# The dummy matmuls that wake TensorE's clock read a preamble constant instead of a zero tile, and are one more

## Chip, cores and metric

One core of a Trainium2 chip. The metric is the device time of one execution in microseconds (us). Every execution also has a span, from the first to the last instruction of the program; it is about 1.8 us shorter than the time.

## The reference, cut

```python
def _A_ref(x, k_cache, v_cache, wq, wo):     # x (1,2048,640); 32 heads of 192; window W = 512
    q = (x @ wq).reshape(B, Sq, Hq, Dh).transpose(0, 2, 1, 3)
    k, v = k_cache[:, :, Sk-W:, :], v_cache[:, :, Sk-W:, :]
    p = softmax(einsum("bhqd,bhkd->bhqk", q, k) * Dh**-0.5)
    return einsum("bhqk,bhkd->bhqd", p, v)...reshape(B, Sq, Hq*Dh) @ wo

def _B_ref(x, w_gate, w_up, w_down):         # 640 -> 1536 -> 640
    return (silu(x @ w_gate) * (x @ w_up)) @ w_down

xn = layernorm(A_x)
return A_x + _A_ref(xn, ...) * silu(_B_ref(xn, ...))
```

## The kernel before

It runs the FFN first, then attention. The FFN's first 512 rows come in four row tiles of 128 (tile 0 to tile 3). A tile's way is: load x, mean and variance on VectorE (two `bn_stats` and a `bn_aggr`), square root on ScalarE, reciprocal and normalisation on VectorE, five transposes on PE, two copies out of PSUM on ScalarE, 30 matmuls of 128 columns. `keep_warm` keeps PE busy in front of that with matmuls whose result is overwritten.

```python
zero_t = ffw.tile([P, 512], bf, name="zero_t")
nc.vector.memset(zero_t[:], 0.0)
...
load_x(0, (nc.scalar, nc.sync))              # a half on each queue
load_x(1, (nc.scalar,))
load_first(slice(0, 2), (nc.sync, nc.scalar))   # gate and up weights, chunks 0-1 of 5
load_first(slice(2, NC))                        # chunks 2-4: "second gate/up weights"
load_x(2, (nc.scalar,))
...
def keep_warm(n, cols=512):
    for _ in range(n):
        nc.tensor.matmul(
            first[2][1][:, 0:cols], zero_t[:, 0:P], zero_t[:, 0:cols], start=True, stop=True
        )

keep_warm(9)
keep_warm(6, P)
...
ln_stats(0)
ln_sqrt(0)
ln_stats(1, lambda: ln_apply(0, (slice(0, 2 * P), slice(2 * P, D))))
ready(0)                                     # transposes and copies of tile 0
...
for t in range(4):
    ...                                      # 30 matmuls per tile; after the first 21 of them:
                    if t < 2:
                        ln_stats(t + 2, lambda: ln_apply(t + 1))
                    ...
                    ready(t + 1)             # transposes of the next tile
```

VectorE, ScalarE and PE each keep this order: the statistics of tile 2 begin before the normalisation of tile 1, and tile 1's transposes stand behind 21 of tile 0's matmuls.

The softmax here doesn't subtract the row's maximum and nothing guards it: scores larger than these inputs give would overflow.

## Time and profile before

| | before |
|---|---|
| median of the time, first 3 runs | 920.73 us (920.32 to 921.08) |
| span of the profiled run | 919.1 us |
| PE busy | 99% of the span |
| first dummy / first real matmul | 1.23 / 6.57 us |
| tile 1's transposes (start of the unbroken stretch) | 8.54 us |

A row of the timeline is start, duration, engine, line, operation, operands, count, and in brackets the idle time before it with what ended it. A row of the chain is start, duration, what. In these rows PE is TensorE, PEld its weight loads, DVE VectorE, ACT ScalarE, SP SyncE and POOL GpSimd; a q behind a name means its queue or sequencer. x_t is a tile of x, stats, mv and rstd are its statistics, xn the normalised tile, tp its transposes in PSUM, xnT the copy of them, wg_sb and wu_sb the gate and up weights, sc and gu their products. Cold and warm stand for TensorE's slow and fast clock, as told apart by how far matmuls start from each other. The prediction shows the lines of before.

### The profile page before, as it was taken

How to read it: one execution, taken by the hardware profiler on the slowest of the kernel's cores; microseconds unless marked ns; L12 is line 12 of the kernel's file. 1: busy time of each engine (PE TensorE's matmuls, PEld its weight loads, DVE VectorE, ACT ScalarE, POOL GpSimd, SP SyncE). 2: the span in 40 equal slices, each digit the busy share in tenths (PEclk: the TensorE clock that was granted, in tenths of full speed). 3: DMA queues.
4: the chain of work that ended last, by engine and by line, in shares of the span. 5: the costliest groups of instructions: out<-in, count | busy, mean ns of one | idle time of the engine just before them, and what ended most of it. 6: DMA issues, size and time to landing. Idle time of an engine off the chain costs nothing.

```text
span 919.1 us, 23152 instructions
## 1 busy us (share of the span) xinstructions
PE 912.6 (99%) x9898; PEld 548.9 (60%) x9920; DVE 601.7 (65%) x844; ACT 474.4 (52%) x840; POOL 85.3 (9%) x269
## 2 busy tenths in 40 slices
PE   9999999999999999999999999999999999999998
PEld 6444444465757575656565656666666666665665
DVE  6443321467777777777777777676867777777657
ACT  4222222556464656565656565655555555556471
POOL 0000000000000000000000000000000000001976
PEclk9999999999999999999999999999999999999999
DMA  9412430045352544263534343435243444343526
GB/s 302 76 34 65 90 84 1 1 75 113 54 113 49 112 51 107 54 109 54 109 58 109 57 109 52 109 54 107 56 85 76 88 79 78 87 71 102 118 61 166
DMA packets 248166, 77.53 MB, mean 84 GB/s; under 512 B 228992, under 2 KB 248064, under 8 KB 248064
## 3 DMA queue, kind: packets, MB, share of 16 engines
q1 hardware_dynamic: 245696, 73.39, 39.5%
q10 hardware_dynamic: 2368, 2.67, 0.9%
q8 instruction: 77, 1.26, 0.6%
q14 instruction: 25, 0.20, 0.1%
HBM read 38.93 MB, written 2.62 MB: 45 GB/s over the span
## 4 chain that ended last, share of the span: by engine, by line
PE 99%; DMA 1%; DVE 0%; ACTq 0%; issue 0%
PE mm L448 22%; PE sc L462 18%; PE mm L487 16%; PE sc L602 15%; PE sc L282 11%; PE mm L312 6%; PE sc L572 4%; PE sc L564 2%; PE mm L539 2%; PE mm L564 1%; DMA x_t<-in_A_x_dram 1%; PE gu L282 0%; PE mm L321 0%; PE sc L539 0%; PE sc L487 0%
## 5 line engine op out<-in xcount | busy, mean ns | idle before, releaser
L466 ACT ACTIVATE p_t<-sc 128x1024 bf16<-128x1024 f32 x254 | 253.0, 1023 | 120.3 <-PE sc L462 120.3
L453 DVE TENSOR_REDUCE qT<-mm 128x512 bf16<-128x1024 f32 x189 | 231.2, 1223 | 99.0 <-PE mm L448 96.5
L517 ACT ACTIVATE O_b<-mm,r 128x192 bf16<-128x192 f32 x486 | 165.0, 422 | 183.1 <-issue 136.6
L448 PE MATMUL mm<-xnT,wq_p 64*128 64x512 bf16 x1890 | 237.5, 376 | 0.0
L462 PE MATMUL sc<-qT,khat 64*128 64x512 bf16 x1524 | 198.0, 376 | 0.0
L487 PEld LDWEIGHTS <-p_t 64*128 64x128 bf16 x3584 | 159.0, 94 | 33.8
L487 PE MATMUL mm<-V_p,p_t 64*128 64x193 bf16 x3520 | 176.4, 243 | 0.0
L615 DVE TENSOR_TENSOR s_m<-s_m,sc 128x1024 f32<-128x1024 f32 x108 | 131.9, 1221 | 60.7 <-PE sc L602 52.3
L602 PE MATMUL sc<-wo_p,OT_b 64*128 64x512 bf16 x1296 | 168.9, 376 | 0.0
L448 PEld LDWEIGHTS <-wq_p 64*128 64x128 bf16 x1890 | 105.0, 94 | 98.9 <-issue 0.8
L462 PEld LDWEIGHTS <-khat 64*128 64x128 bf16 x1536 | 85.3, 94 | 80.4 <-DVE s_t L615 0.3
L602 PEld LDWEIGHTS <-OT_b 64*128 64x128 bf16 x1296 | 70.3, 94 | 44.1 <-issue 0.3
L615 DVE TENSOR_TENSOR s_t<-s_t,sc 128x512 f32<-128x512 f32 x108 | 74.2, 687 | 28.4 <-PE sc L572 26.6
L589 POOL MEMSET turn_t<- 128x1 f32 x220 | 21.6, 98 | 700.0 <-PE mm L487 506.0
L290 DVE TENSOR_TENSOR hT<-sc,sg 128x512 bf16<-128x512 f32 x46 | 31.7, 692 | 81.5 <-ACT sg L289 81.5
L289 ACT ACTIVATE sg<-sc 128x512 bf16<-128x512 f32 x46 | 27.3, 596 | 69.8 <-PE sc L282 66.7
L282 PE MATMUL sc<-xnT,wg_sb 128*128 128x512 bf16 (+1 forms) x255 | 60.1, 354 | 0.5
L282 PE MATMUL sc<-xnT,wu_sb 128*128 128x512 bf16 (+1 forms) x255 | 59.5, 355 | 0.2
L572 PE MATMUL sc<-OT_b,wo_p 64*128 64x512 bf16 (+1 forms) x345 | 50.3, 376 | 0.0
L312 PE MATMUL mm<-wd_sb,hT 128*128 128x512 bf16 x189 | 43.6, 379 | 0.2
L282 PEld LDWEIGHTS <-wu_sb 128*128 128x128 bf16 x285 | 27.1, 98 | 26.8 <-issue 0.3
L282 PEld LDWEIGHTS <-wg_sb 128*128 128x128 bf16 x285 | 27.2, 98 | 26.3
(83 smaller groups left out, 418.3 us busy)
## 6 DMA issues: line engine op xcount, KB each, us to landing
wo_p<-in_A_wo_dram SPq DMA_DIRECT2D x16, 480.0 KB, 4.7
K_p<-in_A_k_cache_dram SPq DMA_DIRECT2D x32, 192.0 KB, 4.4
V_p<-in_A_v_cache_dram SPq DMA_DIRECT2D x32, 192.0 KB, 3.3
wq_p<-in_A_wq_dram SPq DMA_DIRECT2D x64, 80.0 KB, 2.8
wq_p<-in_A_wq_dram SPq DMA_DIRECT2D x16, 160.0 KB, 3.0
x_t<-in_A_x_dram SPq DMA_DIRECT2D x13, 160.0 KB, 3.0
x_b<-in_A_x_dram SPq DMA_DIRECT2D x4, 512.0 KB, 6.1
OT_b<-O_b SPq DMA_TRANSPOSE x124, 2.8
```

Of the source, the lines that this page charges most:

```text
L282: nc.tensor.matmul(out, w_sb[:, c, f * P : (f + 1) * P], xnT[:, c, qc], start=(c == 0), stop=(c == NC - 1),)
L290: nc.vector.tensor_tensor(hTs[b][:, f, :], u, sg[:], ALU.mult)
L312: nc.tensor.matmul(dn, at, by, start=(f == 0), stop=(f == NF - 1))
L448: nc.tensor.matmul(q_ps[:, h, :], pairs[pr]["wq"][r, c, j * P : (j + 1) * P], xnT[r, c, b * 512 : (b + 1) * 512], start=(c == 0), stop=(c ...
L453: nc.vector.reduce_sum(qTs[i][:, j, :], q_ps[:, :, :].rearrange("p h n -> p n h"), axis=AX.X)
L462: nc.tensor.matmul(sc[:, h, :], khat[r, j, ks], qT[r, j, :], start=(j == 0), stop=(j == 2))
L466: nc.scalar.activation(p_t[:, :, :], sc[:, :, :], ACT.Exp, scale=scale)
L487: m = nc.tensor.matmul(acc[:, k, h * 256 : h * 256 + Dh + 1], Ps[i][kc][r, h, qt * P : (qt + 1) * P], V_p[r, kc, h, 0 : Dh + 1], start=(p ...
L517: nc.scalar.activation(O_b[:, qt, h, :], a_k[:, h, 0:Dh], ACT.Copy, scale=r[:, k, h, :])
L572: nc.tensor.matmul(ps.rearrange("p (t q) -> p t q", q=P), pairs[i // NB]["wo"][r, j, MC:D], OTs[i][:, :, :].rearrange("p (t j) q -> p j t ...
L602: m = nc.tensor.matmul(ps[:, k, :], OTs[i][r, 3 * (2 * half + k) + j, :], pairs[i // NB]["wo"][r, j, MAIN], start=(turn == 0 and j == 0), ...
L615: nc.vector.tensor_tensor(to, to, ps, ALU.add)
```

## The change

Its intent: PE need not wait for VectorE's fill, so it can begin to be busy some 0.4 us sooner and its clock is raised sooner; the tenth dummy fills the time won.

```diff
-        zero_t = ffw.tile([P, 512], bf, name="zero_t")
-        nc.vector.memset(zero_t[:], 0.0)
...
         def keep_warm(n, cols=512):
+            ones = [nc.const_aps.tensor(1.0, (P, k), bf) for k in (P, cols)]
             for _ in range(n):
-                nc.tensor.matmul(
-                    first[2][1][:, 0:cols], zero_t[:, 0:P], zero_t[:, 0:cols], start=True, stop=True
-                )
-
-        keep_warm(9)
+                nc.tensor.matmul(first[2][1][:, 0:cols], *ones, start=True, stop=True)
+
+        keep_warm(10)
         keep_warm(6, P)
```

The constant is one bf16 1.0 per partition; a matmul reads it with a step of 0 along its columns, as weights and as moving data.

## The prediction

> **What bounds the kernel now.** I read the page first (busy shares, slices, chain), then the chain over the first 40 us in order of time, then the timeline of the first 9 us, engine by engine, and last a table of two-microsecond windows. The page says that TensorE is the bound of the whole:
>
> ```profile
> PE 912.6 (99%) x9898; PEld 548.9 (60%) x9920; DVE 601.7 (65%) x844; ACT 474.4 (52%) x840; POOL 85.3 (9%) x269
> ...
> PE 99%; DMA 1%; DVE 0%; ACTq 0%; issue 0%
> ```
>
> 99% of the chain that ended last is PE and 1% (some 5 us) is a DMA. So two things can move the end: less matmul work in the body, which the change doesn't touch, or an earlier start of the unbroken stretch of matmuls. The change lies wholly in the first 6 us, so the question is what sets that start. The chain in order of time answers it:
>
> ```profile
> 0.72 0.56 ACTq L188
> ...
> 1.32 0.60 ACTq L188
> ...
> 1.94 0.45 ACTq L193
> ...
> 2.42 4.99 DMA x_t<-in_A_x_dram
> ...
> 7.44 0.49 DVE stats L243
> 7.94 0.07 DVE rstd L265
> ...
> 8.03 0.46 DVE xn L267
> ...
> 8.54 0.45 PE tp L335 x5
> ```
>
> Up to 8.54 us no matmul stands in this chain, neither the dummies nor the first row tile's real ones. It is ScalarE's queue issuing loads, the load of row tile 2 from 2.42 to 7.42 us, the statistics of that tile, and then, because VectorE takes them in this program order, the normalisation of tile 1, which the five transposes at 8.54 wait for. From there PE runs without a break that matters. The timeline of PE shows the slack in front of that point:
>
> ```profile
> 1.23 4.66 PE L230 MATMUL gu<-zero_t 128*128 128x512 bf16 x15 [1.23 <-DVE zero_t L176]
> 5.68 0.74 PE L335 MATMUL tp<-ident,xn 128*128 128x128 bf16 x5
> 6.57 0.27 PE L282 MATMUL sc<-xnT,wg_sb 128*128 128x128 bf16 x1
> ...
> 7.85 0.22 PE L282 MATMUL gu<-xnT,wg_sb 128*128 128x128 bf16 x1
> 8.54 0.45 PE L335 MATMUL tp<-ident,xn 128*128 128x128 bf16 x5 [0.46 <-DVE xn L267]
> ```
>
> The dummies end where tile 0's transposes begin (5.68); tile 0's first 21 matmuls run from 6.57 to 7.85 + 0.22 = 8.07; then PE idles 0.46 us. Anything that PE does sooner or later before 8.07 is first absorbed there.
>
> **What the Trainium skill says.** "TensorE: Matmul & The Clock Gate", Part 1: the array's clock is halved until a free-running window of about 3.4 us has seen it busy, and back-to-back matmuls then go from N/1.2 to N/2.4 + 2.5 ns (427 to 216 ns at 512 columns, 107 to 56 at 128). The trace agrees on the pitches: the dummies' weight loads start at 1.63, 2.06, 2.48 and so on to 5.04, eight steps of 0.426 us, and the first real matmuls start at 6.62, 6.73, 6.84 (0.11 apart), then from 7.02 on 7.07, 7.13, 7.18 (0.055 apart). So the clock was cold through all fifteen dummies and went up at about 6.9 us, some 5.7 us after the first. That is what the dummies are for. The granted clock that the windows print (1.00 throughout) doesn't show this gate; the pitch does. The same page, "Weight-path perf modes": fast weight load asks for 128 weights, an input that isn't FP32, and a column step between -1,023 and 1,024 elements. A broadcast constant has step 0 and stays inside this; no page gives a cost for a step of 0, and no trace of this kernel has one on PE. "Trainium Kernel Development and Optimization", Key Constraints: loads issued from different queues share the same 16 DMA engines. The windows agree: the DMA share is 0.91 to 1.10 from 2 to 16 us, which is why one load of 160 KB takes 4.99 us there.
>
> ```profile
> 2.00:4.00 2.00, 2.00 (x6) 0.76 (x5) 0.50 (x2) 1.06 (x1) 0.00 (x0) 1.00 0.91 242
> 4.00:6.00 2.00, 2.00 (x12) 1.21 (x11) 1.93 (x7) 0.72 (x3) 0.00 (x0) 1.00 1.01 309
> 6.00:8.00 2.00, 1.86 (x25) 1.60 (x23) 1.00 (x4) 0.99 (x3) 0.00 (x0) 1.00 1.04 341
> ```
>
> (The columns: busy time and count of PE, PEld, DVE, ACT, POOL, then granted clock, DMA share, GB/s.)
>
> **The change part by part.**
>
> *Removed: VectorE's fill of the zero tile.* One instruction:
>
> ```profile
> 0.79 0.06 DVE L92 MEMSET one_t<- 128x1 f32 x1 [0.79 <-PEq L842]
> 0.82 0.06 DVE L95 MEMSET eps_t<- 128x1 f32 x1
> 0.90 0.27 DVE L176 MEMSET zero_t<- 128x256 uint32 x1
> 3.50 0.89 DVE L243 BATCH_NORM_STATS2 stats<-x_t 128x6 f32<-128x320 bf16 x2 [2.33 <-DMA x_t<-in_A_x_dram]
> ```
>
> It costs 0.27 us, but VectorE's next work waits for a load until 3.50 after 2.33 us of idling. The idle time becomes about 2.6 us; the statistics don't move. Worth 0 on the path.
>
> *Removed: PE's wait for it.* The first dummy stands at 1.23, of which 0.90 + 0.27 = 1.17 is the end of the fill and 0.06 the handing over. The constant (a bf16 1.0 per partition) is written by POOL at 0.29 us, before the opening barrier, so PE need wait for nothing but the barrier. VectorE, POOL and the two queues come out of it at 0.71 to 0.79. I take 0.80 for PE, an estimate from these starts: 0.43 us earlier.
>
> *Added: one dummy of 512 columns*, at the cold pitch of 0.426 us. The tenth dummy is there to fill exactly the time won. New end of the dummies: 0.80 + 10 x 0.426 + 6 x 0.107 = 5.70, against 1.23 + 9 x 0.426 + 6 x 0.107 = 5.71 before. The transposes of tile 0 start when they did, because their input is done at about 5.5 to 5.8 (VectorE's two halves, 5.20 to 5.84), and the weight load and the matmul count rise by one of some 9,900.
>
> *Moved: when the clock goes up.* PE is busy 0.43 us earlier, so a free-running window can count as busy sooner. If this moves the rise from 6.9 to a window earlier (3.5), the rest of the dummies take half their time and tile 0's transposes and first six matmuls run at 56 instead of 107 ns: 5 x 0.05 + 6 x 0.05, about 0.5 us sooner by 7 us at most. All of it lies ahead of the idle 0.46 us that ends with the normalisation at 8.49, so it only makes that idle time longer. Worth 0 on the path.
>
> *Moved: addresses.* The zero tile's 1,024 bytes per partition go, and the FFN's tiles slide by that much; attention's tiles laid over them later overlap slightly different neighbours. PE gets to attention only after its FFN matmuls, in order, so I see no new wait that could last. Worth 0.
>
> Sum: 0 - 0 + 0 = 0 us; the prediction is the time before, 920.7 us, with perhaps 0.1 us of luck in the clock's phase: 920.6.
>
> **The rivals.** (1) *The earlier dummies shorten the run by what they win*, 0.43 us, so 920.3. For it: the first dummy is the first thing PE does, and PE is 99% of the chain. Against it: the chain has no dummy in it, and the 0.46 us of idling at 8.07 has to be used up by a DMA that comes no sooner. (2) *Reading one element over and over is slow*, or the dummies start later than 0.80. If each of ten dummies took 0.05 us more, they would end at 6.2, tile 0's matmuls would end 0.5 us later, at 8.57, and the slack would be just gone: still 920.7 to 920.8. It takes a doubled pitch (10 x 0.43 us) to cost about 3.8 us, and that is still 0.4%. Nothing in the profile speaks for it. (3) *The clock rises early, the dummies then end a microsecond early, and the pause falls so that the clock drops again.* With a rise at 3.5, dummies end near 4.6 and PE has little to do until 5.6. If it were cold afterwards for a whole window of 3.4 us with PE on the path (8.5 onwards), that window would do half its work: up to 1.7 us, so 922.4. Against it: a pause of 1 us is far short of the window, and the kernel before ran through 0.46 us at 8.07 without a change of pitch. (4) *An effect of the layout*, in either direction, of a few tenths; nothing speaks for it.
>
> **Range and chances.** All four stay within 0.45% of the time, and 2% would be 18.4 us, more than three times all that happens before 6 us. So "within 2%" is all but sure. The range is set by the spread of runs, 920.32 to 921.08 for the kernel before, and by another session's offset of about as much: 919.8 to 921.4. I leave 0.005 each for faster and slower, for what I can't see.
>
> **What would show it.** Right: the first dummy at about 0.8 us with no VectorE wait; its pitch at 0.43 us until the clock rises; tile 0's transposes at 5.6 to 5.8; tile 2's load landing at about 7.4 and tile 1's transposes at about 8.5; PE busy about 0.4 us more. Wrong: tile 1's transposes moved by more than 0.2 us without the load having moved; dummies at a pitch other than 0.43 or 0.22; a pitch of 107 ns after 8.5 us; or any difference in the body beyond 40 us.

## The result, and the profile after

The changed kernel took 921.00 us (median of 6 runs, 920.40 to 922.67), the kernel before 920.81 (6 runs, 920.32 to 921.24); ratio 1.0006, 95% interval 0.9993 to 1.0019: the same. A ratio is the mean time of one kernel's fast runs over that of the other's of the same rounds, so not quite the ratio of the medians. The profiled run of the changed kernel has a span of 918.6 us, half a microsecond under the 919.1 of before. The timeline of the changed kernel, the rows that answer to those of before:

```profile
0.76 4.59 PE L229 MATMUL gu<-const-bfloat16-1.0 128*128 128x512 bf16 x16 [0.76 <-PEq L839]
...
3.54 0.89 DVE L240 BATCH_NORM_STATS2 stats<-x_t 128x6 f32<-128x320 bf16 x2 [2.66 <-DMA x_t<-in_A_x_dram]
...
5.63 0.63 PE L332 MATMUL tp<-ident,xn 128*128 128x128 bf16 x5 [0.29 <-DVE xn L264]
...
6.38 0.22 PE L279 MATMUL sc<-xnT,wg_sb 128*128 128x128 bf16 x1
...
8.04 0.45 PE L332 MATMUL tp<-ident,xn 128*128 128x128 bf16 x5 [0.32 <-DVE xn L264]
```

The first dummy comes 0.47 us sooner and no longer waits for VectorE, whose idle time grew from 2.33 to 2.66 us. The dummies were over before tile 0's normalisation, so its transposes now wait for VectorE (0.29 us), and the first real matmul starts at 6.38 instead of 6.57. The earlier start and VectorE's longer idle time are the change's. The early end of the dummies comes from the clock, which rose while they ran (at 4.7 us, against 6.9 in before); a third trace of before, further down, has its first real matmul at 6.29 with the zero tile. And the half microsecond of the span isn't the change's, as the chain of the same run shows:

```profile
2.42 4.50 DMA x_t<-in_A_x_dram
...
6.94 0.49 DVE stats L240
...
7.53 0.46 DVE xn L264
...
8.04 0.45 PE tp L332 x5
```

Step by step it is the chain of before, shifted: tile 2's load was issued at 2.42 us in both, and took 4.50 instead of 4.99 us. Is the shorter load an effect of the change, or chance? And do the dummies ever stand on the path? These are the questions for the experiments.

### The profile page after: what moved, and what is told of

Its sections match the earlier page's. It is cut to its first block, busy times and chain, and to the rows that moved or that the text cites. A ratio compares the mean times of both kernels' runs of the same rounds, so it can differ in the third digit from the quotient of the medians.

```text
span 918.6 us, 23175 instructions
## 1 busy us (share of the span) xinstructions
PE 913.6 (99%) x9921; PEld 548.6 (60%) x9921; DVE 601.5 (65%) x843; ACT 473.9 (52%) x840; POOL 85.2 (9%) x269
## 4 chain that ended last, share of the span: by engine, by line
PE 99%; DMA 0%; DVE 0%; ACTq 0%; issue 0%
PE mm L445 22%; PE sc L459 18%; PE mm L484 16%; PE sc L599 15%; PE sc L279 11%; PE mm L309 6%; PE sc L569 4%; PE sc L561 2%; PE mm L536 2%; PE mm L561 1%; DMA x_t<-in_A_x_dram 0%; PE gu L279 0%; PE mm L318 0%; PE sc L536 0%; PE sc L484 0%; PE mm L459 0%
```

## The experiments

The theory: the span is decided in the first microseconds by when the loads land; the dummies work beside them. Rival 1: the earlier dummies shorten the run by what they win. Rival 2: reading with a step of 0 is slow. Rival 3: the clock rises early, a pause follows, and it drops again.

All twelve runs gave correct results. They were sent four at a time, each four on one chip with their own runs of the kernel before: 5 rounds each, 3 for the two with 200 dummies, and a single look for the last two. In the table, "clock up" is where the dummies' or matmuls' spacing goes from 0.427 to 0.22 us (512 columns) or from 107 to 56 ns (128); "tile 1" and "tile 3" are the starts of those tiles' transposes in the chain.

| trace | dummies | clock up, us | first real matmul | tile 1 | tile 3 | span | span - tile 3 |
|---|---|---|---|---|---|---|---|
| before, 1st | 9 zero | 6.9 | 6.57 | 8.54 | 12.62 | 919.1 | 906.5 |
| before, 2nd (before_again) | 9 zero | 5.7 to 6.5 | 6.57 | 7.94 | 12.02 | 918.5 | 906.5 |
| before, 3rd (before_third) | 9 zero | 4.0 | 6.29 | 8.82 | 12.90 | 919.5 | 906.6 |
| changed, 1st | 10 ones | 4.7 | 6.38 | 8.04 | 12.12 | 918.6 | 906.5 |
| changed, 2nd (after_again) | 10 ones | 3.8 | 6.35 | 8.20 | 12.28 | 918.8 | 906.5 |
| changed, 3rd (after_third) | 10 ones | 5.1, down, 11.9 | 6.28 | 9.65 | 14.71 | 921.2 | 906.5 |
| ones9 | 9 ones | after 5.1 | 6.30 | 7.85 | 11.93 | 918.4 | 906.5 |
| zero10 | 10 zero | 4.9 | 6.28 | 8.60 | 12.68 | 919.2 | 906.5 |
| none | none | 11.9 | 6.53 | 8.93 | 14.29 | 920.8 | 906.5 |
| apply_first | 10 ones | after 5.5 | 6.49 | 8.36 | 12.35 | 918.9 | 906.6 |
| combo_after | 10 ones | after 5.5 | 6.50 | 7.75 | 12.33 | 918.8 | 906.5 |
| combo_before | 9 zero | after 5.6 | 6.56 | 7.87 | 12.52 | 919.0 | 906.5 |

The last column is the main finding: from tile 3's transposes on, each of these twelve executions took 906.5 or 906.6 us. Whatever tells one from another had happened before about 12 to 15 us.

That the clock is raised sooner, the change's intent, isn't shown: it rose between 3.8 and 5.1 us in the three traces of the changed kernel and between 4.0 and 6.9 in those of before, but in apply_first and combo_after, whose dummies start just as early, only after 5.5. Nor does an early rise decide: before_third has it at 4.0 and the second longest span of the six traces of the two kernels.

### after_again and before_again: each kernel unaltered

> The changed kernel unaltered, for the spread and for a second trace. Theory (the first dummies are off the path; tile 2's load sets the start): ratio to before within 0.9990 to 1.0010; the first dummy at 0.75 us again, but tile 2's load lands anywhere between 6.8 and 7.6 us, and tile 1's transposes start 1.1 us after it, so the half microsecond by which the first trace of the changed kernel began sooner is not of the change. Rival 1 (the earlier dummies shorten the run): the load lands at 6.9 again, and the ratio is 0.9995 or under. Rival 3 (the clock drops again in some runs): some runs over 922, with a pitch of 107 ns after 8 us if the profiled one is such a run.

> The kernel before unaltered, against itself: the noise of this comparison. Theory: ratio 1.0000 with a half-width of the interval of 0.0005 to 0.0010; tile 2's load lands between 6.8 and 7.6 us. Rival 1: lands at 7.4 again, tile 1's transposes at 8.5. Rival 3: if runs over 922 turn up here as well, they are not of the change.

Measured, in the same rounds as before at 921.43 us (9 runs): the changed kernel 921.53, ratio 1.0000 (0.9988 to 1.0013); the kernel before against itself 920.84, ratio 0.9997 (0.9983 to 1.0010). So 0.03% between two copies of one kernel is noise. The interval is also wider than expected, ±0.0013 instead of 0.0005 to 0.0010, or 1.2 us: these ratios can't tell the 0.43 us of rival 1 from nothing. The spans of the same rounds don't show it either: 919.4 us in the mean of the changed kernel's five runs, 919.2 in that of the fourteen of before. Tile 2's load didn't land at 6.9 and 7.4 again but at 7.1 in the changed kernel and at 6.85 in the kernel before: the order is reversed, so the shorter load of the first pair was no steady effect of the change, and I take it for chance.

The chain of the second trace of the kernel before held a surprise:

```profile
0.90 0.28 DVE zero_t L176
...
1.23 4.66 PE gu L230 x15
5.89 0.23 PE tp L335 x2
...
6.14 0.38 ACT xnT L343
...
6.57 0.38 PE sc L282 x4
...
7.94 0.45 PE tp L335 x5
```

Here the loads came early, and what is left is the zero tile's fill, all fifteen dummies, tile 0's transposes and its 21 matmuls. The dummies **are** on the path in this execution.

In the second trace of the changed kernel it is a third thing, the second gate weights that tile 0's 13th matmul needs:

```profile
2.24 5.21 DMA wg_sb<-in_B_w_gate_dram
...
7.50 0.28 PE sc L279 x2
...
8.20 0.45 PE tp L332 x5
```

So tile 1's transposes wait for the latest of three things that often end within a microsecond of each other: tile 2's load (+1.1 us), the second gate weights (+0.7), and PE's own work from the dummies on (first real matmul +1.37; 1.25 and 1.31 in the two combo runs below). Which it is changes from execution to execution.

### ones9 and zero10: one half of the change each

```diff
# ones9: after, with            # zero10: before, with
-keep_warm(10)                  -keep_warm(9)
+keep_warm(9)                   +keep_warm(10)
```

> The constant alone, without the tenth dummy. Theory: first dummy at 0.75 us, the dummies end some 0.2 to 0.43 us sooner than with ten, tile 1's transposes still 1.1 us after tile 2's load; ratio to before within 0.9990 to 1.0010, no different from ten. Rival 1: 0.4 us faster than before, ratio 0.9996. Rival 3: one dummy less makes the pause longer, so more runs over 922.

> The tenth dummy alone, on the zero tile. Theory: first dummy at 1.23 us, dummies end at up to 6.1 us if cold all through, tile 0's first matmul at up to 7.0, its 21st at up to 8.3; the idle time before tile 1's transposes shrinks but does not vanish; ratio within 0.9990 to 1.0010. Rival 1: 0.43 us slower, ratio 1.0005.

Measured against the same 921.43: ones9 920.52, ratio 0.9995 (0.9982 to 1.0007); zero10 920.76, ratio 0.9994 (0.9981 to 1.0006). Neither differs from before, from the whole change, or from the other, as far as ±0.0013 can tell. The tenth dummy on the late-starting zero tile, rival 1's worst case, wasn't seen to be slower; in its trace tile 1's transposes waited for the second gate weights. Its expected late end (up to 6.1 us) didn't occur either, since the clock rose at 4.9 us: the last dummy started at 5.49.

### none: no dummies

```diff
-        keep_warm(10)
-        keep_warm(6, P)
```

> No dummies at all: what they are worth. Theory: PE is idle until tile 0's transposes at about 5.6 us and starts cold, 107 ns a matmul of 128 columns. The clock can rise [...]between 9.0 and 12.5 us. Tile 0's 21 matmuls take 2.2 us instead of 1.2, which is about the slack; tile 1's transposes come 0 to 0.6 us later; after them up to 4 us of cold matmuls lose half of their time. So 0.5 to 2.5 us slower than before: 921.3 to 923.3. Rival: if clock phase never mattered, ratio 1.000.

Measured: 922.48 us against 921.01, ratio 1.0014 (1.0001 to 1.0027), in the middle of the expected range. Its chain:

```profile
8.93 0.53 PE tp L332 x5
9.46 0.21 PE sc L279 x2
...
12.06 0.11 PE gu L279 x2
```

A pair of matmuls takes 0.21 us at 9.46, cold, and 0.11 us at 12.06. The clock rose at 11.9 us, within the expected 9.0 to 12.5. All fifteen dummies together are worth about 1.4 us (1.3 by the mean times, 1.5 by the mean spans; the ratio's interval allows 0.1 to 2.5). That is what the kernel before has already. What starting them sooner can add is something else: the real work that still runs cold, in the first trace of before the five transposes and six matmuls for which the prediction counted 0.5 us, and the few tenths by which the dummies hold up PE where they stand in the chain, as in before_again.

### ones200 and zero200: the cost of one dummy

```diff
# from after / from before
-keep_warm(10)   /  -keep_warm(9)
+keep_warm(200)
```

> 200 dummies of 512 columns on the constant: the cost of one, by itself. Theory: first at 0.75 us, pitch 0.427 us until the clock rises (4.2 to 7.6 us), then 0.216; end at about 46 us, tile 0's transposes right after, tile 1's at about 48.3: 39.5 to 41 us over before, 960 to 962. Rival 2 (a step of 0 is slow to read): a pitch above 0.22 us on the warm clock, and more than 0.5 us above the same on the zero tile.

> 200 dummies on the zero tile, for comparison. Theory: the same as on the constant but for the start 0.45 us later: 960 to 962.5, warm pitch 0.216 us. With PE the bound from its first instruction on, the later start should now show in full: 0.2 to 0.6 us more than on the constant, less or more by the phase in which the clock rises [...]. Rival 2: the constant's is longer by over 0.5 us.

Measured: 961.46 us on the constant, 961.85 on the zero tile (4 runs each, before 921.01; ratios 1.0438 and 1.0442, with intervals of ±0.0015). With so many, PE is the bound from its first instruction, and all of the 40 us show. The summary of the dummies' line in both traces (minimum, median and maximum of their durations in ns, first and last start):

```profile
L229 PE MATMUL gu<-const-bfloat16-1.0 x206: 220/382/631, 0.8 to 46.3; 128*128 128x512 bf16 x100, 128*128 128x128 bf16 x3
```

```profile
L230 PE MATMUL gu<-zero_t x206: 219/379/631, 1.2 to 46.5; 128*128 128x512 bf16 x100, 128*128 128x128 bf16 x3
```

(The shapes at the end are counted on every second matmul.) The medians differ by 3 ns, and so do the distances between starts: between the 20th and the 190th dummy, 218.9 ns each on the constant, 215.8 on the zero tile, without an outlier in either. Cold, both take 426.7 ns. So rival 2 is right in kind and wrong in size: the constant costs 3.1 ns for each warm matmul of 512 columns, 0.6 us over 190 of them, more than the 0.47 us of earlier start. (First to last start is 45.56 and 45.23 us; the difference is smaller than 0.6 because the clock rose at 3.9 us on the constant, 3.1 after the start, and at 4.9 on the zero tile, 3.6 after.) Over ten dummies it is 0.03 us at most. The last six dummies, of 128 columns, are 58 to 60 ns apart on the constant and 55 to 56 on the zero tile: some 3 ns as well, so the cost is one for each matmul and doesn't grow with the columns. It rests on one trace of each. Whether the weights or the moving data pay for it wasn't separated, and neither was the step of 0 from the two other differences, values of 1.0 instead of 0.0 and another address.

The later start of the zero tile, which was to show in full here, doesn't: the medians differ by 0.39 us in the expected direction, within the noise, and the spans of the two traces by 0.3 in the other (959.7 on the constant, 959.4 on the zero tile).

### apply_first: tile 1 no longer waits for tile 2's load

```diff
-                        ln_stats(t + 2, lambda: ln_apply(t + 1))
+                        ln_apply(t + 1)
+                        ln_stats(t + 2)
```

> The changed kernel, with the normalisation of the next tile put ahead of the statistics of the tile after it in VectorE's order, so that tile 1 no longer waits for tile 2's load. Theory: tile 1's normalisation starts at about 7.2 us (after ScalarE's square root), its transposes at about 7.7 instead of 8.0 to 8.5, and PE's unbroken stretch begins up to 0.8 us sooner, unless tile 2's statistics then come late and PE waits there: 919.9 to 920.8, ratio 0.9990 to 1.0000. Rival 1 (the dummies set the start): tile 1's transposes don't move.

Measured: 920.99 against 921.01, ratio 1.0000 (0.9986 to 1.0013). The normalisation of tile 1 started at 7.30 as expected, but its transposes only at 8.36: PE reached tile 0's 13th matmul and waited there for the second gate weights, which landed at 7.64 in this trace:

```profile
7.69 0.28 PE L279 MATMUL sc<-xnT,wg_sb 128*128 128x128 bf16 x2 [0.37 <-DMA wg_sb<-in_B_w_gate_dram]
```

One wait was removed and the next one took its place. The time missed the expected range (919.9 to 920.8), which had left this wait out.

### combo_after and combo_before: both loads taken off tile 1's way

As apply_first, and tile 2's load issued behind the weights:

```diff
         load_first(slice(2, NC))
-        load_x(2, (nc.scalar,))
+        load_x(2)
```

> The changed kernel with both loads taken off the way to tile 1's transposes: the normalisation of tile 1 ahead of tile 2's statistics, and tile 2's load issued behind the first weights on SyncE's queue. In all eight traces so far (but for the two with 200 dummies, and none) the span is the start of tile 1's transposes plus 910.54 to 910.60 us, and that start is the latest of three: tile 2's load + 1.1 us, the second gate weight load + 0.7, or the first real matmul + 1.37. Theory: the weight load comes at 7.3 or sooner, the start is the first real matmul (6.3 to 6.5) + 1.4, 7.7 to 7.9, and the span 918.2 to 918.5; time 919.9 to 920.7, ratio 0.9990 to 1.0000. If the law is wrong, the span doesn't follow that start.

> The same two moves on the kernel before, so with the zero tile and nine dummies. With the loads off the way, the dummies are what is left: they end at 5.68 if the clock is cold all through, so the first real matmul is at 6.57 and tile 1's transposes at 7.94 as in the second trace of the kernel before; if the clock rises early, up to 0.3 us sooner. Theory: span 918.3 to 918.5 by the law, 0 to 0.3 us over the same with the constant; times the same within the noise of 0.1%. Rival 1 (earlier dummies win their 0.43 us in full): 0.4 us over.

Measured: 920.79 and 921.01 against 920.47; ratios 1.0006 (0.9993 to 1.0020) and 1.0007 (0.9994 to 1.0019), where 0.9990 to 1.0000 was expected of the first. Tile 1's transposes started at 7.75 and 7.87, as expected from PE's own work alone, the constant 0.12 us ahead of the zero tile. But the rule that I had put down (span = tile 1's transposes + 910.55) fell: the spans were 911.1 us after them. The chain of combo_after shows why:

```profile
3.26 4.45 DMA x_t<-in_A_x_dram
...
7.74 0.90 DVE stats L240 x2
...
8.66 0.22 DVE mv L243
...
8.90 0.29 ACT rstd L253
9.20 0.38 ACT xnT L340
...
9.61 0.38 PE sc L279 x4
```

Tile 2's load now lands at 7.72, and its square root stands on ScalarE ahead of a copy that tile 1's matmuls need. PE now waits until 9.61, for tile 1's matmuls, and no longer at 8. Put in terms of tile 3 instead of tile 1 the rule holds for these two as well (last column of the table). In combo_before the load landed 0.19 us later, and its span is 0.2 longer: again a load, not the dummies. No version here beats the two kernels.

### after_third and before_third: one more look each

> A third trace of the changed kernel. Law: span = start of tile 1's transposes + 910.55; the start is the latest of tile 2's load + 1.1, the second gate weights + 0.7, the first real matmul + 1.37 us, and which of the three it is differs from trace to trace. First dummy at 0.76; the clock rises between 4.2 and 5.8 us.

> A third trace of the kernel before. The same law; first dummy at 1.23; first real matmul at 6.57 if the clock stays cold up to 5.6, sooner if not. If the start of tile 1's transposes lies between 7.9 and 8.6 us again, the traces of before and after overlap and the change has no mark of its own in the span.

The third trace of before has a span of 919.5, tile 2's load landing at 7.70. The third trace of the changed kernel took 923.18 us, span 921.2, and shows rival 3 at work. Its chain:

```profile
2.23 6.23 DMA wg_sb<-in_B_w_gate_dram
...
8.51 0.39 PE sc L279 x2
...
9.65 0.53 PE tp L332 x5
...
14.71 0.28 PE tp L332 x5
```

Its wait for the second gate weights in the timeline, and the same row of zero10, where the clock stayed up:

```profile
8.51 0.39 PE L279 MATMUL sc<-xnT,wg_sb 128*128 128x128 bf16 x2 [1.40 <-DMA wg_sb<-in_B_w_gate_dram]
```

```profile
7.89 0.28 PE L282 MATMUL sc<-xnT,wg_sb 128*128 128x128 bf16 x2 [0.79 <-DMA wg_sb<-in_B_w_gate_dram]
```

The windows of the changed kernel's third and first trace for 8.5 to 15 us (busy us and count of PE, PEld, DVE, ACT, POOL; then granted clock, DMA share, GB/s):

```profile
8.50:15.00 6.50, 6.49 (x88) 6.49 (x89) 3.48 (x12) 2.01 (x7) 0.00 (x0) 0.74 1.10 335
```

```profile
8.50:15.00 6.50, 6.50 (x112) 6.24 (x110) 3.00 (x10) 4.46 (x11) 0.00 (x0) 1.00 1.10 335
```

The second gate weights landed at 8.46, about 1 us later than in the second trace. PE had done twelve of tile 0's matmuls by 7.11 us and then had nothing to do for 1.4 us. When it went on, the spacing was 107 ns until 11.8 us: the clock, up at 5.1, had dropped. It was back at 11.9. From the 13th matmul to tile 3's transposes this trace took 14.71 - 8.51 = 6.20 us, the second one 12.28 - 7.50 = 4.78: the drop cost 1.42 us, the late weights 8.51 - 7.50 = 1.01. Together that is the 2.4 us between the two spans.

**Does the change make this more likely?** This stays open. Of the changed kernel's 12 executions whose span is known, five have a span of 920.0 us or more; of 33 of the unaltered kernel before, in the experiments, none has (919.9 at most). But I chose that line after seeing the runs, and chips differ. And of the 15 executions of ones9, apply_first and combo_after, which start their dummies just as early, none is above 919.6. A cause in the change isn't shown, and nor is its absence.

## Why the prediction was right or wrong

**The time** (920.6 predicted, 921.0 measured, range 919.8 to 921.4): right, and "no difference" held in every comparison of the unaltered kernels and of the two halves. This alone says little for the reasoning: with intervals of ±0.13%, or 1.2 us, any effect of half a microsecond would have come out as no difference too. What follows rests on the traces.

**The removed fill** is worth nothing on VectorE, as predicted: its next instruction still waits for the load.

**The earlier start**: 0.80 predicted, 0.76 measured. **The tenth dummy** costs 0.427 us cold, as predicted. That the dummies would end at 5.70, as before, was wrong: the last one started at 5.13, 4.70 and 5.34 in the three traces of the changed kernel, as the clock rose during them (cold all through, it would have been 5.6). The prediction had this as a possibility, with the consequence that it lengthens idle time further on. That holds where a load comes last, in five of the six traces of the two kernels, and not where PE's own work does.

**"In this chain no matmul stands"** was true of the trace that I had, and I took it for a property of the kernel. It isn't: of three traces of before, one has the fill and all the dummies in its chain. "A DMA that comes no sooner" failed in the same way: tile 2's load landed anywhere between 6.7 and 8.0 us in the unaltered kernels and ones9. The second gate weights, the last to come in two of the three traces of the changed kernel, weren't in the prediction at all. The conclusion survived, with some luck, because the loads are mostly the later ones, and where they aren't, PE's own work allows only some 0.2 us (first real matmul at 6.28 to 6.38 in the three traces of the changed kernel, 6.57, 6.57 and 6.29 in those of before), under the noise.

**Rival 1** (0.43 us in full, a ratio of 0.9995) isn't excluded by the times: their intervals include it. The traces speak against it: what the change moves on PE's side is a few tenths up to the first real matmul, and in five of the six traces of the two kernels a load ends the wait after it. **Rival 2** exists, at 3.1 ns a matmul instead of the 50 that I tried out, if it is the step that costs them. **Rival 3** I had argued away too quickly ("a pause of 1 us is far short of the window"). It did happen once, and with it a sign that the prediction had named as speaking against itself, 107 ns after 8.5 us. But it came in another way than I had drawn it: the dummies ran up to tile 0's transposes without a pause (5.56 and 5.54 us), and the pause of 1.4 us lay in tile 0's matmuls, before weights that landed late. Its size of up to 1.7 us was right (1.42), and the late load added its own 1.0. **The layout's shift** had no effect: after tile 3 all executions take the same 906.5 us, with the zero tile and without.

## What to carry to other kernels

Before speeding up the head of a chain, take several traces of the same kernel: where three waits end within a microsecond of each other, one trace's critical chain names only the one that happened to be last. Find the point from which all executions take the same time (here tile 3's transposes), and ask of any change whether it moves that point. What dummy matmuls that wake the clock are worth is measured by taking them out (here about 1.4 us); what starting them sooner can still win is another sum, the real work that runs cold in spite of them. Look at both first.

## What the Trainium skill lacked or had wrong

- "TensorE: Matmul & The Clock Gate", "Why this matters for your kernels", advises against idle gaps of more than some 3 us between bursts of matmuls. Here the clock dropped after a single gap of about 1.4 us (7.1 to 8.51 us) between short bursts. In zero10 PE idled 0.8 us at the same place (7.11 to 7.89) and the clock stayed up. Whether the longest gap decides or the busy time of a whole window isn't shown, since they go together here: in the 3.4 us after the rise PE was busy for 1.90 us in after_third and for 2.50 in zero10.
- The same page, Part 1, puts the rise at some 4 us into activity, with a spread of 500 ns, but also calls it run-variable. Here it came between 2.8 us (before_third: 4.0 after a start at 1.23) and 5.7 us (before) after the first dummy, and in none 6.2 us after the first transpose. The window's length that it gives, 3.4 us, agrees: in after_third the clock rises at 5.1 us, is down just as work resumes at 8.51, and is back at 11.9, two stretches of about 3.4 us each.
- The same page gives no cost for an operand read with a step of 0. Here a warm matmul of 512 columns took 218.9 ns on the constant against 215.8 on the zero tile, with no difference on the cold clock (426.7 ns both); that the step is the cause isn't separated from the values and the address.
- No page says what the profile's granted clock shows of this gate: it stays at 1.00 while the clock is cold at the start of the kernel, and shows a later drop (0.74 for 8.5 to 15 us in after_third).
